# Attention and mixer kernel: batch 0's mixer as one stretch ahead of batch 2's attention, with seven products in all its blocks, and three of its x tiles in other buffers

## The chip, the cores and the metric

The kernel runs on 1 core of one Trainium2 chip. The metric is the device time of one execution in microseconds (us), given as the median of several runs. A core has five engines, each with its own instruction queue worked off in order: TensorE (PE in the profile, its weight loads PEld), VectorE (DVE), ScalarE (ACT), GpSimd (POOL) and SyncE (SP). In this kernel SP's queue issues every transpose by DMA and every store of the output; POOL's queue issues the loads of u, z, v and the weights.

## The reference

There are 8 batches of 3008 rows; u and v have 256 columns, z has 64. A gated attention makes x, and a mixer of two products in a row works on x:

```
scores = (z @ z.T) / 3008
x   = u * (maximum(scores, 0)**2 @ v)
h   = maximum(x.T @ w_tok1, 0) @ w_tok2          # 256 token features
u2  = x + h.T
out = u2 + maximum(u2 @ w_ch1, 0) @ w_ch2        # 1536 channel features
```

Nothing crosses from one batch to another, so the mixer of one batch may be done while the attention of a later one runs.

## The kernel before

**Tiles.** A batch is cut into six blocks q = 0 to 5 of 512 columns of rows (the last of 448), and its keys into six groups of four tiles of 128 rows. Operands are bf16; sums are in the eight banks of the PSUM, as slots of two banks that scores, attention sums, mixer products and their evacuations take in turn. A slot is free again when the instruction that empties it has run, on ScalarE or VectorE.

**Attention.** For a block and a key group, `score_run` (L465) multiplies two halves of z against each other at once; ScalarE takes relu to `at` (L491, L503), VectorE squares it (L511, L542). Scores are symmetric, so a group below the diagonal isn't computed again: `flip` (L562) lets SP transpose the `at` of its mirror image into a buffer `fl` (11 of them), and on the diagonal `flip_tiles` (L554) fills the lower triangle in three transposes within `at`. The attention's second product (L692, `acc`) uses `at` or `fl` as the moving side. Its two sums, one for each half of the 128 output rows, are joined by a copy on ScalarE and an add on VectorE (`cp`, L820, L826); the `gate` (L846, L851) multiplies by `uT`, the u rows transposed by SP (`turn_u`, L265, from `ur`), and writes x, transposed, to a tile `xT` (9 buffers). The planner issues a gate when `uT` has been asked for; the time of its landing isn't looked at.

**Mixer.** `turn_x` (L884, `x_pair`) turns x back by SP, `x_sums` (L921) makes sums and differences of it on VectorE, and the token product runs in seven products instead of eight (`tok1`, L1029, `a_ps`). VectorE collects it (`collect_a`, L1045 to L1063, `a_f`, `a_sb`), `tok2` (L1086, `h_ps`) makes h, and VectorE adds it into xT (L1095), from which SP makes `u_sb` (L1114). The channel half is `ch1` (L1143, `hp`), an evacuation with relu to `h2pre` (L1182 on ScalarE, L1184 on VectorE), and the second product in one of two forms. The plain one (`ch2`, L1366, `op`) is 48 matmuls of 128x256 a block, and VectorE adds u (L1383, `res`). The other first makes four sums of each four h2 tiles on VectorE (`make_sums`, L1223 to L1235, `hsum`) and then runs seven products of 12 matmuls of 128x128 each, 84 a block (L1280, `xb` and `zb`), which VectorE adds up into `ro` in seven adds (L1317). Which form a block takes is said by `fast(q)`: every block of batches 1 to 7 but the very last, and blocks 3 to 5 of batch 0, take the seven products.

**Order.** A planner written in the kernel emits the whole order of instructions. It goes through the attention's blocks, keeps a clock of each engine with assumed costs (a flip takes SP 2.2 us and lands 6.5 us after that, for example), puts pieces of the mixer (lists `heads` and `tails`) between the halves of the attention, and queues work for the other engines by the times that it assumes. `goals` says how far the mixer may go from the beginning of a block of the attention on; what it lets in is put ahead of that block's further work. A key (b, n) stands for step n of batch b's mixer: (0, 0) is batch 0's `tok1`, and (0, 4) lets in its `tok2` and the channel half of blocks 0 to 2. The before kernel lets batch 0's `tok1` in from batch 1's block 2 on, (0, 4) from batch 1's block 3 on, and the rest of batch 0 from batch 2's first block on. Loads are asked for by `at_group`, counted in key groups: those of z for batch 2 at the end of batch 1's block 2 (`ask_z`), each followed by its transpose `zT` (L141, L145). A load on POOL's queue waits behind a small marker operation (`mark`, L124) that holds it back until the work at that place has run.

Two rules of the before kernel concern only this place: in batch 1 the scores may not run further ahead than one block (`n = 0` in the main loop), and sums for the first seven-product block of a batch may be put off (`late_sums`).

Of the kernel before, what the change touches and what calls it, by code (L numbers as in the profile page):

```python
# [9 lines left out]
BF16 = mybir.dt.bfloat16  # L10
# [3 lines left out]
P = 128  # L14
QW = 512
# [42 lines left out]
def kernel(  # L58
# [12 lines left out]
    B, S, D = u.shape  # L71
# [7 lines left out]
    CHT = d_ch // P  # L79
    DT = D // P  # L80
# [288 lines left out]
    def has_room(names):  # L369
        return names() if callable(names) else all(live[n] < ROOM[n] for n in names)  # L370
# [279 lines left out]
    def do_whole(start, g):  # L650
        blk = cur[0]
        begins = blk.g is None
        if begins:
            blk.g, blk.half = g, 0
            blk.todo.remove(g)
            blk.slot += 1
            blk.parts.setdefault(g, 2 if g == LAST else 1)
            n = grain(blk.b, blk.q, g)
            tiles = list(range(GK - 1 if g == LAST else GK))
            blk.steps = [(dh, tiles[i:i + n]) for i in range(0, GK, n) for dh in range(DT)]  # L660
        final = blk.slot == NG
        if begins:
            if final and not blk.tails:
                do_tails(blk, max(start, tails_ready(blk)))
                start = pe[0]
        dh, tiles = blk.steps[blk.half]
        start, end = on_pe(start, "full", len(tiles) * column_time(blk.W))
        for i in tiles:
            whole_matmul(blk, g, i, dh, final and i == tiles[-1])
        if final:  # L670
            acc_free[dh] = push(
                "dve", end + 0.21, 0.61, 0.75,
                lambda t, dh=dh: gate(blk, dh, blk.acc[dh], t), first=1,
                room=("xT",) if dh == 0 else lambda: (blk.b, blk.q) in xTs)
        blk.half += 1
        if blk.half == len(blk.steps):
            blk.g = None
            finished(blk, g)
            if final:
                end_block(blk)  # L680
                if blk.q == WHOLE - 1:
                    ring.append((acc_free[-1], RING))
# [121 lines left out]
    def finish(blk, dh, end):  # L804


        W, acc = blk.W, blk.acc[dh]
        summed = Done()
        guess[blk.home[dh]] = end + 1.7
        ring.append((summed, blk.home[dh]))  # L810

        def load(e):
            return max(free[e], end) + sum(op.busy for op in waiting[e])

        on_act = blk.b > 0 or load("act") + 0.46 < load("dve") + 0.67

        def copy(t):
            cp = sb.tile([P, QW], F32, tag="res", name="cp", bufs=3)
            if on_act:
                nc.scalar.copy(cp[:, :W], acc[:, 1, :W])  # L820
            else:
                nc.vector.tensor_copy(cp[:, :W], acc[:, 1, :W])
            push("dve", t, 0.66, 0.78, lambda t: add(cp, t), first=1, done=summed)

        def add(cp, t):
            nc.vector.tensor_add(cp[:, :W], acc[:, 0, :W], cp[:, :W])  # L826
            push("dve", t, 0.58, 0.7, lambda t: gate(blk, dh, cp, t), first=1,
                 room=(lambda: (blk.b, blk.q) in uTs and has_room(("xT",))) if dh == 0
                 else lambda: (blk.b, blk.q) in xTs)

        engine, busy = ("act", 0.46) if on_act else ("dve", 0.66)
        push(engine, end + 0.21, busy, busy + 0.15, copy, first=1)

    gated = [0]

    def gate(blk, dh, acc, t):
        b, q, W = blk.b, blk.q, blk.W
        uT = uTs[b, q]
        if dh == 0:
            xTs[b, q] = sb.tile([P, DT, QW], BF16, tag="xT", name="xT", bufs=ROOM["xT"])  # L840
            live["xT"] += 1
            if W < QW:
                nc.gpsimd.memset(xTs[b, q][:, :, W:], 0.0)
        xT = xTs[b, q]
        full, rest = W // P, W % P
        nc.vector.tensor_mul(  # L846
            xT[:, dh, :full * P].rearrange("p (t s) -> p t s", s=P),
            acc[:, :full * P].rearrange("p (t s) -> p t s", s=P),
            uT[:, :full, dh, :])
        if rest:  # L850
            nc.vector.tensor_mul(  # L851
                xT[:, dh, full * P:W], acc[:, full * P:W], uT[:, full, dh, :rest])
        if dh == DT - 1:
            if b == 0 and q > 1:
                release("fl", [1], t)
            gated[0] += 1
            push("sp", t, 1.25, 7.5 if q < NQ - 1 else 12.0, lambda t: turn_x(b, q, t),
                 first=1 if b == 0 or q >= NQ - 2 else -1,
                 room=x_room(b, q), frees=fl_free if b and q % 2 == 0 else ())
# [139 lines left out]
    def add_mixer(b):  # L999
# [110 lines left out]
        def turn_u2(q, t):  # L1110
            live["us"] += 1
            turned_back[b] += 1
            us = sb.tile([P, DT, QW // P, P], BF16, tag="res", name="u_sb", bufs=3)
            nc.sync.dma_start_transpose(  # L1114
                out=us.rearrange("p h t d -> p (h t) d"),
                in_=xTs[b, q].rearrange("p h s -> p (h s)"))
            st["u", q] = us
            release("xT", xT_uses[q])
            for waits in st.pop(("waits", q), []):
                waits(t)  # L1120

# [8 lines left out]
        def ch1(q, c2, borrowed, end):  # L1130
# [28 lines left out]
            if (b, q, c2) == VERY_LAST:  # L1159
                landed, freed = [], Done()  # L1160

                def evacuate_part(r, t):
                    if r:
                        nc.scalar.activation(h2[:, r, :W], hps[1][:, r, :W], ACT.Relu)
                    else:
                        nc.vector.tensor_single_scalar(h2[:, r, :W], hp[:, r, :W], 0.0, AX.max)
                    landed.append(t)
                    if len(landed) == 2:
                        h2_done[q, c2].t = freed.t = max(landed)
                        keep_ends()  # L1170

                for r, engine, at, busy in ((0, "dve", end - 0.18, 0.62), (1, "act", end + 0.21, 0.5)):
                    push(engine, at, busy, busy + 0.16, lambda t, r=r: evacuate_part(r, t))
                ring.extend((freed, slot) for slot in slots)
                release("xT", xT_uses[q])
                return
            on_act = load("act") + 0.92 < load("dve") + 1.15 + (b > 0)

            def evacuate(t):
                recent[0] = h2[:, 0, :1]  # L1180
                if on_act:
                    nc.scalar.activation(h2[:, :, :W], hp[:, :, :W], ACT.Relu)  # L1182
                else:
                    nc.vector.tensor_single_scalar(h2[:, :, :W], hp[:, :, :W], 0.0, AX.max)  # L1184
                if q == NQ - 1:
                    keep_ends()
                if fast(q) and c2 % 2:
                    if borrowed and q == HALF and b < B - 1:
                        late_sums.append(lambda t: make_sums(q, c2 // 2, t))
                    else:  # L1190
                        make_sums(q, c2 // 2, t)
# [1 line left out]
            ring.append((push(engine, end + 0.21, busy, busy + 0.16, evacuate,  # L1193
                              done=h2_done[q, c2]), slots[0]))
            if c2 == CHT // 2 - 1:
                release("xT", xT_uses[q])

        def pairs_of(q):

# [146 lines left out]

        def fast(q):

            return (b > 0 or q >= HALF) and (b, q) != (B - 1, NQ - 1)

        def ch2(q, half, i, end):
            apart = alone(q, half)
# [138 lines left out]
    def next_piece(t):  # L1491
# [6 lines left out]
        for l in lists:  # L1498
            if not l:
                continue  # L1500
            p = l[0]
            if not p.urgent and p.key > goal[0]:
                continue
            if p.opens and not p.closes and opened and not (p.joins and joined[0]):
                continue
            r = max(t, known(*p.needs))
            if p.room and not has_room(p.room):
                r = FAR
            if p.slot:
                r = max(r, min(slots)) if slots else FAR  # L1510
            if r < FAR and r <= t + 0.05:
                return r, l
            if r < best[0]:
                best = r, l
# [79 lines left out]
            lambda: used.get((b, vorder[j]), 0) == NQ)  # L1594

    HALF = NQ // 2

    def ask_u(m, group):
        at_group(group, lambda: ask(lambda: u_then_turn(m), lambda: len(uTs) > m - 2))
# [6 lines left out]
    for b in range(B):  # L1606
# [15 lines left out]
                    at_group(base + NG + 4 + j // 3, lambda b=b, j=j: turn_next_z(b, j // 3))  # L1622
        else:
            if b == 1:
                ask_z(2, base + HALF * NG - 1)
            if b + 1 < B:
                last, m = base + NQ * NG - 1, (b + 1) * NQ
                ask_u(m, last)
# [102 lines left out]
    late_z(5, 9.0)  # L1731
    first_u(18.5)

    goals = {(1, 2): (0, 0), (1, HALF): (0, 1 + HALF)}
    for b in range(2, B):
        goals[b, 0] = (b - 1, 1 + HALF)
    done_units = 2
    NOW = 0.05
    STARVED = 0.7
# [3 lines left out]
    while cur[0] is not None or heads or tails:  # L1743
# [16 lines left out]
        runs = blk is not None and blk.whole  # L1760
        most = RING if runs else 1
        n = can_score(done_units, most)
        if n and blk is not None and blk.b == 1:
            b, q, _ = units[done_units][0]
            if b * NQ + q > NQ + blk.q + 1:
                n = 0
        slots = sorted(d.t for d, _ in ring if d.t is not None)
        n_now = min(n, len(slots))
        ts = FAR
# [115 lines left out]
```

## Time and profile before

| | |
|---|---|
| time, median of 3 runs | 1116.05 us (1115.90 to 1116.34) |
| the profiled execution | 1116.06 us |
| its span in the trace | 1114.0 us |
| TensorE busy | 1108.1 us, 10965 matmuls |
| VectorE busy | 780.5 us, 1855 instructions |
| ScalarE busy | 655.1 us, 817 instructions |
| GpSimd busy | 162.7 us, 382 instructions |
| mean granted clock of TensorE | 1.00 |

The span runs from the first instruction to the last in the trace; the execution lies some 2.1 us around it. Busy times are sums over the whole span. The mean duration of a pipelined matmul in the groups (375 ns for 512 columns) is longer than the time from its start to the next one's start, so the pace of a run of matmuls is read from the chain, which gives the length of a run and how many matmuls are in it. A row of the timeline gives the start, the length, the engine, the source line and what the instruction writes and reads; "SPq" is SP's queue. The length of a transpose there is that of its issue on SP, not of its transfer.

In the trace, batch 0's `tok1` begins at 110.4 us, its `tok2` at 127.8, and the plain channel half of blocks 0 to 2 runs from 134.8 to 166.0; then comes batch 1's attention from its block 3 on.

### The profile page before, as it was taken

How to read it: one execution, taken by the hardware profiler on the slowest of the kernel's cores; microseconds unless marked ns; L12 is line 12 of the kernel's file. 1: busy time of each engine (PE TensorE's matmuls, PEld its weight loads, DVE VectorE, ACT ScalarE, POOL GpSimd, SP SyncE). 2: the span in 40 equal slices, each digit the busy share in tenths (PEclk: the TensorE clock that was granted, in tenths of full speed). 3: DMA queues.
4: the chain of work that ended last, by engine and by line, in shares of the span. 5: the costliest groups of instructions: out<-in, count | busy, mean ns of one | idle time of the engine just before them, and what ended most of it. 6: DMA issues, size and time to landing. Idle time of an engine off the chain costs nothing.

```text
span 1114.0 us, 26933 instructions
## 1 busy us (share of the span) xinstructions
PE 1108.1 (99%) x10965; PEld 675.6 (61%) x10965; DVE 780.5 (70%) x1855; ACT 655.1 (59%) x817; POOL 162.7 (15%) x382
## 2 busy tenths in 40 slices
PE   9999999999999999999999999999999999999998
PEld 3444574666557665576555865557655576556676
DVE  6889846875758757588566885578756787557775
ACT  8999524645854458545675356653666536743354
POOL 5321100211003110031000311003200120000000
PEclk9999999999999999999999999999999999999999
DMA  9999955796987979779597897868968678585213
GB/s 178 173 183 157 208 117 114 124 179 135 183 137 142 187 126 185 142 141 209 128 174 132 143 197 144 168 121 158 191 156 172 109 157 174 128 160 99 63 58 95
DMA packets 466155, 165.51 MB, mean 149 GB/s; under 512 B 433072, under 2 KB 449008, under 8 KB 466032
## 3 DMA queue, kind: packets, MB, share of 16 engines
q1 hardware_dynamic: 436640, 131.11, 58.0%
q0 software_dynamic: 28880, 32.32, 20.6%
q8 instruction: 85, 1.39, 0.5%
q10 hardware_dynamic: 512, 0.38, 0.1%
q14 instruction: 38, 0.31, 0.1%
HBM read 65.40 MB, written 24.64 MB: 81 GB/s over the span
## 4 chain that ended last, share of the span: by engine, by line
PE 97%; DVE 1%; ACT 1%; issue 1%; POOL 0%; DVEq 0%; POOLq 0%; ACTq 0%
PE acc L692 41%; PE hp L1143 21%; PE xb L1280 10%; PE zb L1280 7%; PE sc L465 6%; PE h_ps L1086 4%; PE a_ps L1029 3%; PE op L1366 3%; PE first_acc L609 1%; DVE a_f L1045 0%; ACT h2pre L1182 0%; PE wp L205 0%; ACT at L503 0%; POOL hs L1156 0%; DVE at L511 0%
## 5 line engine op out<-in xcount | busy, mean ns | idle before, releaser
L1182 ACT ACTIVATE h2pre<-hp 128x1024 bf16<-128x1024 f32 (+1 forms) x277 | 269.4, 1007 | 257.8 <-PE hp L1143 165.3
L692 PEld LDWEIGHTS <-v_sb 64*128 64x128 bf16 x4418 | 238.0, 94 | 219.3
L692 PE MATMUL acc<-at,v_sb 64*128 64x512 bf16 (+1 forms) x2738 | 338.8, 374 | 0.0
L503 ACT ACTIVATE at<-sc 128x1024 bf16<-128x1024 f32 (+1 forms) x290 | 287.5, 1027 | 72.2 <-PE sc L465 65.4
L511 DVE TENSOR_TENSOR at<-at 128x1024 bf16<-128x1024 bf16 (+1 forms) x290 | 198.5, 687 | 110.7 <-ACT at L503 106.7
L1143 PE MATMUL hp<-xT,w_ch_sb 128*128 128x512 bf16 (+1 forms) x1152 | 273.5, 375 | 0.1
L692 PE MATMUL acc<-fl,v_sb 64*128 64x512 bf16 (+1 forms) x1680 | 191.4, 367 | 0.0
L1143 PEld LDWEIGHTS <-w_ch_sb 128*128 128x128 bf16 x1152 | 106.2, 98 | 99.8 <-issue 3.0
L465 PE MATMUL sc<-zT 64*128 64x512 bf16 (+1 forms) x732 | 131.3, 360 | 0.1
L1280 PEld LDWEIGHTS <-hsum 128*128 128x128 bf16 x1944 | 115.9, 98 | 17.6 <-issue 1.1
L1280 PEld LDWEIGHTS <-h2pre 128*128 128x128 bf16 x1458 | 89.1, 98 | 19.3 <-issue 1.2
L820 ACT COPY cp<-acc 128x512 f32<-128x512 f32 (+1 forms) x94 | 54.9, 584 | 71.4 <-PE acc L692 59.8
L826 DVE TENSOR_TENSOR cp<-acc,cp 128x512 f32<-128x512 f32 (+1 forms) x94 | 63.5, 675 | 42.3 <-ACT cp L820 41.8
L491 ACT ACTIVATE at<-sc 128x512 bf16<-128x512 f32 (+3 forms) x152 | 56.1, 444 | 45.4 <-PE sc L465 45.0
L1223 DVE TENSOR_TENSOR hsum<-h2pre 128x512 bf16<-128x512 bf16 (+1 forms) x132 | 52.2, 400 | 37.7 <-ACT h2pre L1182 35.9
L1280 PE MATMUL xb<-w_mix_sb,hsum 128*128 128x128 bf16 x972 | 68.6, 219 | 0.4 <-DVE ro L1317 0.3
L542 DVE TENSOR_TENSOR at<-at 128x512 bf16<-128x512 bf16 (+3 forms) x152 | 41.5, 321 | 38.3 <-ACT at L491 38.2
L1317 DVE TENSOR_TENSOR ro<-xb,u_sb 128x256 f32<-128x256 f32 (+1 forms) x132 | 52.6, 399 | 21.9 <-PE xb L1280 20.2
L465 PEld LDWEIGHTS <-zT 64*128 64x128 bf16 x732 | 42.0, 94 | 41.8 <-issue 3.8
L124 POOL CAST mark<-at 128x1 f32<-128x1 bf16 x24 | 8.9, 369 | 375.2 <-DVE at L511 375.2
L846 DVE TENSOR_TENSOR xT<-cp,uT 128x512 bf16<-128x512 f32 (+1 forms) x94 | 62.4, 664 | 0.8
L1095 DVE TENSOR_TENSOR xT<-xT,h_ps 128x1024 bf16<-128x1024 bf16 (+1 forms) x48 | 54.6, 1172 | 4.7 <-PE h_ps L1086 4.6
(89 smaller groups left out, 983.0 us busy)
## 6 DMA issues: line engine op xcount, KB each, us to landing
out_dram<-ro SPq DMA_DIRECT2D x37, 512.0 KB, 2.9
v_sb<-in_v_dram POOLq DMA_DIRECT2D x40, 256.0 KB, 4.6
ur<-in_u_dram POOLq DMA_DIRECT2D x40, 256.0 KB, 5.1
w_tok_sb<-in_moe_w_tok_dram POOLq DMA_DIRECT2D x10, 256.0 KB, 10.7
zs<-in_z_dram POOLq DMA_DIRECT2D x35, 64.0 KB, 3.7
at<-at SPq DMA_TRANSPOSE x114, 2.4
out_dram<-ro SPq DMA_DIRECT2D x7, 256.0 KB, 2.2
fl<-at SPq DMA_TRANSPOSE x105, 4.4
```

The costliest lines, as they stand in the source:

```text
L465: nc.tensor.matmul(sc[:, r, c0:c1], zT[h, k:k + P], zT[h, m + c0:m + c1], start=True, stop=True)
L491: nc.scalar.activation(a3[:, i, c0:c1], sc[:, r, c0:c1], ACT.Relu, scale=inv_S)
L503: nc.scalar.activation(view, sv, ACT.Relu, scale=inv_S)
L511: nc.vector.tensor_mul(view, view, view)
L692: nc.tensor.matmul(o, vs[blk.b, g][rows, i, dh * P:(dh + 1) * P], rhs, start=(dh, h) not in blk.begun, stop=stop, skip_group_check=True)
L820: nc.scalar.copy(cp[:, :W], acc[:, 1, :W])
L826: nc.vector.tensor_add(cp[:, :W], acc[:, 0, :W], cp[:, :W])
L846: nc.vector.tensor_mul(xT[:, dh, :full * P].rearrange("p (t s) -> p t s", s=P), acc[:, :full * P].rearrange("p (t s) -> p t s", s=P), uT[: ...
L1095: nc.vector.tensor_add(to, to, h[:, :, :n * P].rearrange("p h (s t) -> p h t s", t=n))
L1143: nc.tensor.matmul(hps[r % len(hps)][:, r, :W], w_ch1_sb[:, dc, cc * P:(cc + 1) * P], xT[:, dc, :W], start=(dc == 0), stop=(dc == DT - 1))
L1182: nc.scalar.activation(h2[:, :, :W], hp[:, :, :W], ACT.Relu)
L1280: nc.tensor.matmul(to[:, i * P:(i + 1) * P], lhs, weights[:, c2, :], start=(first_use and c2 == 0 and i == 0), stop=(c2 == CHT // 2 - 1), ...
```

## The change

- Batch 0's `tok1` is let in from batch 1's block 5 on, and all the rest of batch 0's mixer where batch 2's attention begins, as one stretch ahead of it. Batch 1's `tok1` is held back until the last block of batch 0's mixer.
- Blocks 0 to 2 of batch 0 take the seven products as well.
- Since all of batch 0's x has to be kept longer, three x tiles get another home: block 0's is the buffer `hs`, those of blocks 1 and 2 share one `fl` buffer (`x_kept`); the others stay in `xT`.
- The loads of z for batch 2 are asked for 13 key groups earlier (`Z2` = 4 instead of 17), and the rule that held batch 1's scores to one block ahead goes.
- Sums are put off only in batches 1 and up.

```diff
@@ -671,7 +671,7 @@
             acc_free[dh] = push(
                 "dve", end + 0.21, 0.61, 0.75,
                 lambda t, dh=dh: gate(blk, dh, blk.acc[dh], t), first=1,
-                room=("xT",) if dh == 0 else lambda: (blk.b, blk.q) in xTs)
+                room=xT_room(blk.b, blk.q) if dh == 0 else lambda: (blk.b, blk.q) in xTs)
         blk.half += 1
         if blk.half == len(blk.steps):
             blk.g = None
@@ -825,20 +825,53 @@
         def add(cp, t):
             nc.vector.tensor_add(cp[:, :W], acc[:, 0, :W], cp[:, :W])
             push("dve", t, 0.58, 0.7, lambda t: gate(blk, dh, cp, t), first=1,
-                 room=(lambda: (blk.b, blk.q) in uTs and has_room(("xT",))) if dh == 0
+                 room=(lambda: (blk.b, blk.q) in uTs and has_room(xT_room(blk.b, blk.q))) if dh == 0
                  else lambda: (blk.b, blk.q) in xTs)
 
         engine, busy = ("act", 0.46) if on_act else ("dve", 0.66)
         push(engine, end + 0.21, busy, busy + 0.15, copy, first=1)
 
     gated = [0]
+    x_kept = {}
+
+    def new_xT(b, q):
+
+        if b or q > 2:
+            xTs[b, q] = sb.tile([P, DT, QW], BF16, tag="xT", name="xT", bufs=ROOM["xT"])
+            live["xT"] += 1
+        elif q == 0:
+            hs = sb.tile([P, CHT, P], BF16, tag="hs", name="x_hs", bufs=1)
+            xTs[b, q] = hs.rearrange("p c s -> p (c s)")[:, :DT * QW].rearrange(
+                "p (h s) -> p h s", h=DT)
+        else:
+            if q == 1:
+                x_kept["fl"] = sb.tile(
+                    [P, 2, DT, QW], BF16, tag="fl", name="x_kept", bufs=ROOM["fl"])
+                live["fl"] += 1
+                fl_free.pop(0)
+            xTs[b, q] = x_kept["fl"][:, q - 1]
+
+    def xT_room(b, q):
+
+        return ("xT",) if b or q > 2 else ("fl",) if q == 1 else ()
+
+    x_kept_uses = [2]
+
+    def done_with_xT(b, q, uses):
+
+        uses[0] -= 1
+        if uses[0]:
+            return
+        if b or q > 2:
+            live["xT"] -= 1
+        elif q:
+            release("fl", x_kept_uses, pe[0] + 0.2)
 
     def gate(blk, dh, acc, t):
         b, q, W = blk.b, blk.q, blk.W
         uT = uTs[b, q]
         if dh == 0:
-            xTs[b, q] = sb.tile([P, DT, QW], BF16, tag="xT", name="xT", bufs=ROOM["xT"])
-            live["xT"] += 1
+            new_xT(b, q)
             if W < QW:
                 nc.gpsimd.memset(xTs[b, q][:, :, W:], 0.0)
         xT = xTs[b, q]
@@ -1115,7 +1148,7 @@
                 out=us.rearrange("p h t d -> p (h t) d"),
                 in_=xTs[b, q].rearrange("p h s -> p (h s)"))
             st["u", q] = us
-            release("xT", xT_uses[q])
+            done_with_xT(b, q, xT_uses[q])
             for waits in st.pop(("waits", q), []):
                 waits(t)
 
@@ -1172,7 +1205,7 @@
                 for r, engine, at, busy in ((0, "dve", end - 0.18, 0.62), (1, "act", end + 0.21, 0.5)):
                     push(engine, at, busy, busy + 0.16, lambda t, r=r: evacuate_part(r, t))
                 ring.extend((freed, slot) for slot in slots)
-                release("xT", xT_uses[q])
+                done_with_xT(b, q, xT_uses[q])
                 return
             on_act = load("act") + 0.92 < load("dve") + 1.15 + (b > 0)
 
@@ -1185,7 +1218,7 @@
                 if q == NQ - 1:
                     keep_ends()
                 if fast(q) and c2 % 2:
-                    if borrowed and q == HALF and b < B - 1:
+                    if borrowed and q == HALF and 0 < b < B - 1:
                         late_sums.append(lambda t: make_sums(q, c2 // 2, t))
                     else:
                         make_sums(q, c2 // 2, t)
@@ -1193,7 +1226,7 @@
             ring.append((push(engine, end + 0.21, busy, busy + 0.16, evacuate,
                               done=h2_done[q, c2]), slots[0]))
             if c2 == CHT // 2 - 1:
-                release("xT", xT_uses[q])
+                done_with_xT(b, q, xT_uses[q])
 
         def pairs_of(q):
 
@@ -1346,7 +1379,7 @@
 
         def fast(q):
 
-            return (b > 0 or q >= HALF) and (b, q) != (B - 1, NQ - 1)
+            return (b, q) != (B - 1, NQ - 1)
 
         def ch2(q, half, i, end):
             apart = alone(q, half)
@@ -1501,6 +1534,8 @@
             p = l[0]
             if not p.urgent and p.key > goal[0]:
                 continue
+            if p.key == (1, 0) and tails and tails[0].key < (0, 1 + NQ):
+                continue
             if p.opens and not p.closes and opened and not (p.joins and joined[0]):
                 continue
             r = max(t, known(*p.needs))
@@ -1594,6 +1629,7 @@
             lambda: used.get((b, vorder[j]), 0) == NQ)
 
     HALF = NQ // 2
+    Z2 = 4
 
     def ask_u(m, group):
         at_group(group, lambda: ask(lambda: u_then_turn(m), lambda: len(uTs) > m - 2))
@@ -1622,7 +1658,7 @@
                     at_group(base + NG + 4 + j // 3, lambda b=b, j=j: turn_next_z(b, j // 3))
         else:
             if b == 1:
-                ask_z(2, base + HALF * NG - 1)
+                ask_z(2, base + Z2)
             if b + 1 < B:
                 last, m = base + NQ * NG - 1, (b + 1) * NQ
                 ask_u(m, last)
@@ -1731,9 +1767,8 @@
     late_z(5, 9.0)
     first_u(18.5)
 
-    goals = {(1, 2): (0, 0), (1, HALF): (0, 1 + HALF)}
-    for b in range(2, B):
-        goals[b, 0] = (b - 1, 1 + HALF)
+    goals = {(b, 0): (b - 1, 1 + HALF) for b in range(2, B)}
+    goals[1, NQ - 1] = (0, 0)
     done_units = 2
     NOW = 0.05
     STARVED = 0.7
@@ -1760,10 +1795,6 @@
         runs = blk is not None and blk.whole
         most = RING if runs else 1
         n = can_score(done_units, most)
-        if n and blk is not None and blk.b == 1:
-            b, q, _ = units[done_units][0]
-            if b * NQ + q > NQ + blk.q + 1:
-                n = 0
         slots = sorted(d.t for d, _ in ring if d.t is not None)
         n_now = min(n, len(slots))
         ts = FAR
```

## The prediction

> **What bounds the kernel now.** The page's first part and the engine line of its chain of waits come first.
>
> ```profile
> PE 1108.1 (99%) x10965; PEld 675.6 (61%) x10965; DVE 780.5 (70%) x1855; ACT 655.1 (59%) x817; POOL 162.7 (15%) x382
> ...
> PEclk9999999999999999999999999999999999999999
> ...
> PE 97%; DVE 1%; ACT 1%; issue 1%; POOL 0%; DVEq 0%; POOLq 0%; ACTq 0%
> ```
>
> TensorE is busy for 1108.1 of 1114.0 us at full granted clock and is 97% of the chain. So a matmul taken away is a full gain, and a wait put in front of TensorE is a full loss: nothing later gives it back. The question is what the new order of matmuls costs in matmuls, and whether what feeds them can keep that order.
>
> The chain in order of time, in the old mixer stretch of batch 0 and in a block that already uses seven products, gives prices:
>
> ```profile
> 126.13 1.73 PE acc L692 x16
> ...
> 139.94 5.24 PE op L1366 x48
> 145.18 5.18 PE hp L1143 x24
> ...
> 201.54 2.75 PE hp L1143 x12
> 204.29 0.67 PE xb L1280 x12
> ```
>
> One attention matmul is 1.73/16 = 0.108 us, one plain channel matmul (`op`) 5.24/48 = 0.109 us, one product matmul 0.67/12 = 0.0558 us.
>
> The timeline of SP's queue, which issues every transpose, is the third view (start, length, tile, count):
>
> ```profile
> 106.27 12.99 SPq L562 DMA_TRANSPOSE fl<-at  x4
> 119.42 1.24 SPq L265 DMA_TRANSPOSE uT<-ur  x1
> 120.71 14.02 SPq L562 DMA_TRANSPOSE fl<-at  x5
> 134.85 2.83 SPq L1114 DMA_TRANSPOSE u_sb<-xT  x2
> 137.78 1.25 SPq L265 DMA_TRANSPOSE uT<-ur  x1
> ...
> 158.40 2.54 SPq L141 DMA_TRANSPOSE zT<-zs  x2
> ...
> 167.47 3.76 SPq L554 DMA_TRANSPOSE at<-at  x3
> 171.33 2.10 SPq L562 DMA_TRANSPOSE fl<-at  x1
> ```
>
> From 106 to 139 us the queue hardly rests. A small transpose takes 1.29 us from start to start (three `at` pieces: 167.47 to 171.33), a flip alone 2.1, four flips while u is loaded 13.15/4 = 3.3. Before the change nobody waits for this, because its mixer stretch (126 to 166 us) follows, where few transposes are asked for and the late ones are worked off.
>
> **The work, step by step.** Blocks 0, 1 and 2 of batch 0 lose 3 x 48 = 144 `op` matmuls: 144 x 0.1092 = 15.72 us. They gain 3 x 84 = 252 product matmuls: 252 x 0.0558 = 14.07. Net **-1.65 us**. The order of TensorE's instructions is the same for the first 937 matmuls (to 110.37 us, where `a_ps` began before) and for the last 9250 (from 201.54). In between, one stretch instead of two pieces takes away two changes between attention and mixer matmuls at about 0.1 us of idle each, and perhaps the 0.3 us for which `hp` waited at 201.54: together -0.5.
>
> VectorE gains 3 x (12 sums `hsum` + 7 adds `ro`, 0.42 us each) less the six `res` adds (0.69): +19.8 us in all, none on TensorE's path as long as VectorE stays ahead. A fast block is 5.18 + 84 x 0.0558 = 9.87 us of TensorE against 19 x 0.42 + 1.22 (the `u` add) = 9.2 of VectorE, so cover remains, 0.7 us a block. ScalarE's six `h2pre` of 1.0 us are covered too. The x tiles in `hs` and in one flip buffer add no instruction; they take one of 11 flip buffers for some 60 us. Priced at nothing; if a flip then waits for a buffer, that is in the transposes' lateness below. Output DMAs: three fewer in batch 0, no consumer.
>
> So far: profiled execution 1116.06 (span 1114.0, median of runs 1116.05) - 1.65 - 0.5 = **1113.9**, if TensorE never waits.
>
> **What SP's queue is asked for.** The attention of batch 1's blocks 2 to 4 now follows at once, 40 us earlier than the last of it did, and its flips, triangle pieces and u transposes with it; z of batch 2, whose `zT` stood at 143.9 to 162, now comes in the same stretch: six `zs` loads move ahead of the u loads on POOL's queue, five transposes on SP's. In order after the flip that began at 117.17 in the trace of before (the last one common to both orders): flip, `zT` x2, flip, flip, `at`, `zT` x3, flip, `at`, then flip **F** (for block (1,3)), `at`, flip, `at` x3, **U3** (uT of block (1,3)), `at` x3, **U4** (uT of block (1,4)). No such pile stands in the trace, so I add it up from rows:
> - F starts at 117.2 + 5 flips x 2.3 + 7 small x 1.29 + two u loads (993rd and 1031st matmul) at 2.2 each (the flip beside the load at 119.25 took 4.25 instead of 2.1) = **142**; with 2.1 per flip and 1 per load 138.7, with 2.4 and 3.3 per load 144.8. I take 141.5, since small transposes leave the DMA engines room for part of a load.
> - U3 is issued F + 2.1 + 1.29 + 2.1 + 3.87 = F + 9.4 and lands 3.0 later (row of `uT`: shortest 2.7, median 3.3): **153.9**.
> - U4 is issued 5.2 after U3, lands at 159.1. The next u load waits for U3's landing and then falls on it: 0 to 3 us, I take 1.5: **160.6**.
>
> **Who waits.** Block (1,3)'s gate stands in VectorE's order with its landing of U3, and (1,4)'s with U4; VectorE works in order, so all behind it waits too. Behind gate (1,3): the two `cp` adds that free the accumulators for block (1,5), whose first matmul would stand at 110.37 + (283 + 39) x 0.108 + 0.5 (nine small scores) + 84 x 0.0558 = 150.3 without waits. It can start at U3 + 2 gates x 0.69 + add 0.69 + 0.2 = 156.2. Behind gate (1,4): the last two sums of `a_f` that empty the bank of `tok1`, which the score after 28 more matmuls (153.0 without waits) takes: U4 + 2 x 0.69 + 2 x 0.42 + 0.1 = 162.9, so TensorE is **9.9 us** late there. Waits on the way (F itself wanted at 141.9, landing near 146; the second `zT` wanted at 138.4) are part of the 9.9, not added to it: SP and DMA run on while TensorE waits. After it, `tok2` (160.8 without waits) needs nothing further of SP, and TensorE is the bound again.
>
> Sum: 1113.9 + 9.9 = 1123.8. Bounds of the wait: from F at 138.7 with no load on U4, 138.7 + 17.6 + 2.3 - 153.0 = 5.6; from F at 144.8 and the whole load, 14.7. My sums leave TensorE no credit for transposes that overlap better than before, so I go 0.8 below and forecast **1123.0**.
>
> **Rivals.**
> - Transposes keep up: 1113.9. For it: in before nothing ever waited for a transpose, and the order gives U4 14 us from its place to its use. Against: in before SP ran 4 to 10 us behind its places with fewer of them in the stretch. The same case would be slower by 0.2% only from a wait of 4.3 us upward. Chance 0.13. (An edit that does not do what it says is out: the new order has the 252 products and the single stretch.)
> - SP catches up partly, a wait of 1.5 to 5 us at F or U3 only: F begins at 134.5 to 137, when flips and loads overlap fully. 1115.4 to 1118.9. Chance 0.14.
> - VectorE becomes the bound in the three new fast blocks: transposes in time, but x sums (8 x 0.29 us a block) come on top of 9.2 in 9.87, so TensorE waits 1 to 3 us: 1115 to 1117. Against: at 200 to 269 us VectorE is busy 76% with the same blocks, and the `hp` wait was 0.3. Chance 0.05.
> - A long wait also slows the clock: in the trace the granted clock is 1.00 throughout, but no wait of TensorE reached 1 us after the start, so no run here shows what several us do. If the matmuls after each of two such waits ran at half pace for as long as two passes of `acc` x16 (3.46 us), each would cost 1.7: 1123.0 + 3.4 = 1126.4. Chance 0.1. The Trainium skill (TensorE: Matmul & The Clock Gate, "Part 1: The HAM clock gate") states such a rule: about 3.4 us without matmuls bring the clock to half until some 3.4 us of them have run. By it the forecast would be near 1126; that is the rival just priced, and the trace neither bears it out nor speaks against it.
>
> **How the numbers follow.** Forecast (wait of 5 to 13 us) 0.58, keep up 0.13, partly 0.14, VectorE 0.05, clock 0.10. A measurement of this kernel can tell about 0.2%, 2.2 us: faster is below 1113.8, slower above 1118.3. Keep-up lies on the first edge: faster 0.07, same 0.06. Of partly, two thirds are same; VectorE is same. Faster 0.07, same 0.20, slower 0.73. The range 1115.3 to 1127.5 leaves out keep-up and the upper clock cases, under 0.2; the forecast's own is 1119 to 1127.
>
> **What would show it.** In the profile after, groups: `xb`/`zb` 252 matmuls more, `op` 144 fewer, PE busy 1.6 lower. SP's timeline from 106 to 165 us without a gap. DVE's `xT` (gate) with idle ahead, released by DMA `uT`; a gap of TensorE at about 142 to 160 before `acc` and `sc`, and none after. Wrong if those gates find uT landed, if SP has gaps before 140 us, or if the losses stand in the mixer stretch behind `hsum`.

## The result and the profile after

The changed kernel takes 1123.57 us (median of 6 runs, 1121.99 to 1129.55) against 1116.19 of the kernel before in the same runs: the ratio is 1.0071, 95% interval 1.0044 to 1.0098. It is slower, by 5 to 11 us. The profiled execution took 1121.99 us, its span is 1120.0, so 6.0 us more than before between the first instruction and the last. It is the fastest of the six executions; what the 1.6 us between it and the median are, its trace can't say.

The page after, engines and granted clock (the chain's share of TensorE is now 93%, with 3% for DMA):

```profile
PE 1105.4 (99%) x10999; PEld 679.7 (61%) x11073; DVE 787.8 (70%) x1899; ACT 662.6 (59%) x824; POOL 169.8 (15%) x382
...
PEclk9999899999999999999999999999999999999999
...
PE 93%; DVE 3%; DMA 3%; ACT 1%; issue 1%; SPq 0%; POOL 0%; DVEq 0%; ACTq 0%; POOLq 0%
```

The weight loads count the matmuls: 11073 against 10965, 252 products more and 144 `op` fewer; 74 records of matmuls themselves are missing from this trace. One digit of the clock row is 8, which no digit was before.

Where the 6.0 us come from is read by laying the weight loads of both kernels side by side, since no record of them is missing. At 109 us, where the order is still the same, they are 0.1 us apart. Where the common order begins again (201.5 us before, 208.5 after) the changed kernel is 7.0 behind; 0.7 of that comes back at 627 and 764 us, where the kernel before has two short waits that the changed one hasn't, and 0.3 at the end. With the 1.65 us of work saved, waits and what hangs on them cost some 8.6 us in between. Taking each matmul's time to the next one's start, less its pace (by the rows in the prediction 55.8, 109.2 and 215.8 ns for 128, 256 and 512 columns), places them: 0.6 in two waits at 109 and 111 us, **6.8 from 128 to 139**, 0.6 in two near 160, 0.9 at 193; the kernel before loses some 0.4 more than the changed one in the rest of the stretch. The large one is a wait and what follows it. TensorE's timeline of the kernel after, with what ended the wait in brackets:

```profile
127.59 1.04 PE L692 MATMUL acc<-at,v_sb 64*128 64x512 bf16 x8
132.58 0.58 PE L465 MATMUL sc<-zT 64*128 64x512 bf16 x2 [3.95 <-ACT at L503]
132.88 1.56 PE L692 MATMUL acc<-at,v_sb 64*128 64x512 bf16 x6
134.16 0.42 PE L465 MATMUL sc<-zT 64*128 64x256 bf16 x2
134.35 1.94 PE L692 MATMUL acc<-at,v_sb 64*128 64x512 bf16 x8
```

A score waits 4.1 us (128.45 to 132.58), and then eight `acc` matmuls take 1.94 us where they took 1.04. ScalarE's timeline shows whom it waited for:

```profile
126.52 0.55 ACT L491 ACTIVATE at<-sc 128x256 bf16<-128x256 f32 x2 [0.48 <-PE sc L465]
131.51 1.94 ACT L503 ACTIVATE at<-sc 128x1024 bf16<-128x1024 f32 x2 [4.44 <-DMA fl<-at]
```

The relu had its scores, but no `at` buffer to write to. There are six, and a buffer is free again only when the flip that reads it has landed. Between 100 and 172 us ScalarE waits 5.6 us for flips in all; in the kernel before it waits for none there. That flip is in SP's timeline, and the u load beside it in GpSimd's:

```profile
106.89 13.08 SPq L562 DMA_TRANSPOSE fl<-at  x5
120.14 2.55 SPq L141 DMA_TRANSPOSE zT<-zs  x2
122.81 8.03 SPq L562 DMA_TRANSPOSE fl<-at  x2
...
141.14 1.63 SPq L562 DMA_TRANSPOSE fl<-at  x1
...
149.72 2.14 SPq L265 DMA_TRANSPOSE uT<-ur  x1
...
155.83 1.26 SPq L265 DMA_TRANSPOSE uT<-ur  x1
```

```profile
118.70 0.57 POOL L255 DMA_DIRECT2D ur<-in_u_dram  x1 [0.33 <-issue]
122.80 0.54 POOL L255 DMA_DIRECT2D ur<-in_u_dram  x1 [0.33 <-issue]
```

The first of the two flips at 122.81 alone took SP 5.94 us and landed at 131.41; the u load issued at 122.80 landed at 128.94, and the one of 118.70 at 124.96. A flip alone took 1.63 (141.14). The windows of the same trace show the clock (columns: TensorE's busy time, weight loads, VectorE, ScalarE, GpSimd, granted clock, DMA share, GB/s):

```profile
130.00:132.00 2.00, 0.00 (x0) 0.00 (x0) 0.00 (x0) 0.49 (x1) 0.00 (x0) 0.89 1.16 207
132.00:134.00 2.00, 1.42 (x8) 0.81 (x9) 1.43 (x3) 1.88 (x3) 0.00 (x0) 0.50 0.57 128
134.00:136.00 2.00, 2.00 (x13) 0.89 (x10) 2.00 (x8) 1.10 (x4) 0.00 (x0) 0.50 1.22 163
...
138.00:140.00 2.00, 2.00 (x20) 0.99 (x18) 1.34 (x6) 0.16 (x1) 0.00 (x0) 0.90 0.66 148
```

The granted clock falls to 0.50 within the wait, at 131.56, and is back at 138.38. From 132.58 to 138.30 TensorE does work that takes 3.0 us at the pace of before; it takes 5.7. The half clock costs 2.7 us on top of the 4.1.

### The profile page after: what moved, and what is told of

Read it like the earlier page. It is cut to its first block, busy times and chain, and to the rows that moved or that the text cites. A ratio compares the mean times of both kernels' runs of the same rounds, so it can differ in the third digit from the quotient of the medians.

```text
span 1120.0 us, 27125 instructions
## 1 busy us (share of the span) xinstructions
PE 1105.4 (99%) x10999; PEld 679.7 (61%) x11073; DVE 787.8 (70%) x1899; ACT 662.6 (59%) x824; POOL 169.8 (15%) x382
## 4 chain that ended last, share of the span: by engine, by line
PE 93%; DVE 3%; DMA 3%; ACT 1%; issue 1%; SPq 0%; POOL 0%; DVEq 0%; ACTq 0%; POOLq 0%
PE acc L692 39%; PE hp L1176 21%; PE xb L1313 10%; PE zb L1313 8%; PE sc L465 6%; PE h_ps L1119 4%; PE a_ps L1062 3%; DMA fl<-at 1%; PE op L1399 1%; PE first_acc L609 1%; DVE at L511 1%; DMA uT<-ur 1%; DMA v_sb<-in_v_dram 1%; ACT at L503 1%; DVE a_f L1078 0%
## 5 line engine op out<-in xcount | busy, mean ns | idle before, releaser
L1215 ACT ACTIVATE h2pre<-hp 128x1024 bf16<-128x1024 f32 (+1 forms) x284 | 276.3, 1008 | 256.1 <-PE hp L1176 170.4
L692 PEld LDWEIGHTS <-v_sb 64*128 64x128 bf16 x4418 | 241.7, 94 | 217.8 <-issue 2.7
L1176 PE MATMUL hp<-xT,w_ch_sb 128*128 128x512 bf16 (+1 forms) x1020 | 254.4, 374 | 3.2
L1313 PEld LDWEIGHTS <-hsum 128*128 128x128 bf16 x2088 | 124.5, 98 | 19.3 <-issue 1.3
L1313 PEld LDWEIGHTS <-h2pre 128*128 128x128 bf16 x1566 | 95.6, 98 | 20.8 <-issue 1.2
L1256 DVE TENSOR_TENSOR hsum<-h2pre 128x512 bf16<-128x512 bf16 (+1 forms) x141 | 56.1, 402 | 38.5 <-ACT h2pre L1215 36.5
L1313 PE MATMUL xb<-w_mix_sb,hsum 128*128 128x128 bf16 x1044 | 73.6, 219 | 0.8 <-DVE ro L1350 0.8
L1350 DVE TENSOR_TENSOR ro<-xb,u_sb 128x256 f32<-128x256 f32 (+1 forms) x141 | 56.4, 400 | 22.5 <-PE xb L1313 20.6
L124 POOL CAST mark<-at 128x1 f32<-128x1 bf16 x29 | 13.1, 453 | 381.3 <-DVE at L511 381.1
L1268 DVE TENSOR_TENSOR hsum<-h2pre,hsum 128x512 bf16<-128x512 bf16 (+1 forms) x141 | 56.4, 400 | 2.2
```

Source lines behind the costliest of these rows:

```text
L692: nc.tensor.matmul(o, vs[blk.b, g][rows, i, dh * P:(dh + 1) * P], rhs, start=(dh, h) not in blk.begun, stop=stop, skip_group_check=True)
L1176: nc.tensor.matmul(hps[r % len(hps)][:, r, :W], w_ch1_sb[:, dc, cc * P:(cc + 1) * P], xT[:, dc, :W], start=(dc == 0), stop=(dc == DT - 1))
L1268: nc.vector.tensor_sub(kind(3), tiles_of(q, d, 1, 0), kind(1))
L1313: nc.tensor.matmul(to[:, i * P:(i + 1) * P], lhs, weights[:, c2, :], start=(first_use and c2 == 0 and i == 0), stop=(c2 == CHT // 2 - 1), ...
L1350: nc.vector.tensor_add(res(m, h), source, us(m, h) if opening else res(m, h))
```

## The experiments

The theory from this profile: SP's queue is late, as forecast, but it stops TensorE in more places than the two gates, because three kinds of buffers are free only when a transfer has landed (`at` by flips, the gates' cp tiles by uT, `ro` by stores). The waits stand side by side, and the one that ends last at each point counts. The rivals: the u loads alone; the early z alone; VectorE in the new fast blocks. The ratios are to the kernel before, run in between on the same chip, with 95% intervals. The spread of single runs is wide (the changed kernel's 7.6 us), so that a difference of two ratios under 0.2% tells little, and the trace decides more than the time.

**u_quarter and u_half.** In the load of u:

```diff
-        nc.gpsimd.dma_start(out=ur[:, :n, :], in_=rows_of(u[b], q))
+        if (b, q) in ((1, 3), (1, 4)):
+            nc.gpsimd.dma_start(out=ur[:, :1, :], in_=rows_of(u[b], q)[:, :1, :])
+            nc.gpsimd.memset(ur[:, 1:, :], 0.0)
+        else:
+            nc.gpsimd.dma_start(out=ur[:, :n, :], in_=rows_of(u[b], q))
```

(u_half: two tiles instead of one.)

> The changed kernel with the same order on TensorE, VectorE, ScalarE and SP; only the two u loads of batch 1's blocks 3 and 4 move a quarter of their bytes (the other three tiles of ur are set to zero, so this part of the output is left out). Theory: TensorE's wait of 4.13 us at 128.2 is ScalarE's relu waiting for an at buffer, which the flip issued at 122.81 holds until it lands at 131.4; the flip took 8.6 us because a u load ran beside it, and the half clock until 138 follows from the wait. Then the flip lands some 3 to 4 us earlier, the wait is under 1 us, no slice of the granted clock is under 1, and the time is 1115 to 1117. Rival 1, the two zT transposes put in front of the flip are the cause: the flip is still late by 2.5 us, wait 2 to 4 us. Rival 2, the wait comes from VectorE or ScalarE being behind: wait and clock unchanged, 1122 or more.

> As u_quarter, with half of the bytes of those two u loads (half of ur set to zero, so this part of the output is left out). Theory: the flip lands 1.5 to 2.5 us earlier, the wait at 128 is 1.5 to 2.5 us, and since it is shorter than 3.4 us the granted clock stays at 1.00: 1116.5 to 1119. Were the half clock tied to any wait, some matmuls after it would still run at half pace. Rivals as for u_quarter.

Measured: u_quarter 1.0055 (1.0035 to 1.0076), u_half 1.0071 (1.0052 to 1.0091): about as slow as the changed kernel. The trace tells why. TensorE's waits in u_quarter:

```profile
129.99 0.37 PE L469 MATMUL sc<-zT 64*128 64x512 bf16 x2 [0.77 <-ACT at L507]
160.33 0.41 PE L469 MATMUL sc<-zT 64*128 64x512 bf16 x2 [4.16 <-DVE a_f L1082]
```

The first part held: the wait at 128 fell from 4.1 to 0.9 us, since the flip took SP 2.67 us instead of 5.94. The two `zT` transposes still stood ahead of it, so rival 1 is out. The time didn't follow, because another wait took its place. VectorE's gates in the same run:

```profile
150.47 1.29 DVE L883 TENSOR_TENSOR xT<-cp,uT 128x512 bf16<-128x512 f32 x2 [3.41 <-DMA uT<-ur]
158.45 1.29 DVE L883 TENSOR_TENSOR xT<-cp,uT 128x512 bf16<-128x512 f32 x2 [4.37 <-DMA uT<-ur]
```

They wait for uT of (1,3) and (1,4), and the score that needs the bank of `tok1` behind them begins at 160.33; in the changed kernel it began at 161.22, in u_half at 161.06. It is nearly the same point in all three, whatever TensorE lost before, but not because SP's queue stood alike. SP issued the transpose for (1,4) 3.0 us earlier in u_quarter than in the changed kernel:

```profile
152.87 1.25 SPq L269 DMA_TRANSPOSE uT<-ur  x1
```

It landed at 158.43, 5.6 us after its issue instead of 3.5: the next u load, which waits for the landing of (1,3)'s uT, was issued in two parts from 150.93 on and landed at 154.75 and 157.40. A transpose beside a load is late once more; without that load it was not tried. A half clock of 3.4 us follows it now. My expectation of 1115 to 1117 had forgotten the second wait, which the prediction had. u_half shows the same, with a wait of 4.1 before 161.06; it lost the half clock at 128 but has it at 161. Its first wait came out at two of 0.7 and 0.9, each less than the 1.5 to 2.5 expected.

**uT_first and uT_first_u_quarter.** In the turn of u:

```diff
-            "sp", pe[0], 1.25, 5.0, lambda t: turn_u(m // NQ, m % NQ, t))))
+            "sp", pe[0], 1.25, 5.0, lambda t: turn_u(m // NQ, m % NQ, t), first=2 if m < 2 * NQ else 0)))
```

> The changed kernel with one edit: the planner puts the transposes of u for batch 1 ahead of other waiting transposes in SP's queue, so that uT of blocks (1,3) and (1,4) stands 5 and 12 operations earlier. Theory, two chains run side by side and the later one sets the end: the flip that holds ScalarE's at buffer (4.1 us and half clock) is in front of these operations and stays, only the 0.6 us at 160 go: 1120.5 to 1123. Rival, the gates' wait for uT is the cause and the wait at 128 only takes its place: the time falls by 3 us or more.

> Both edits together: u transposes first, and a quarter of the bytes in the u loads of blocks (1,3) and (1,4) (the rest of ur zero, that part of the output left out). Theory: u_quarter took away the wait at 128 and showed the one behind the gate of (1,4); uT_first takes that away too, so no wait of TensorE between 105 and 170 us is above 1.5 us, no half clock, 1115 to 1117.5. Rival, SP's queue is late by a fixed amount that always comes out somewhere: another wait of 3 us or more turns up before 170 us and the time stays above 1119.

Measured: uT_first 1.0081 (1.0055 to 1.0108), which speaks against the rival's fall of 3 us; its trace keeps a wait of 3.9 us behind a flip at 136.7. It has another of 3.3 at 108.2, which is not the edit's: the u loads of the start came late in this execution (see plain_blocks below). Both edits together: **1.0013 (0.9997 to 1.0030)**, 1119.27 us. Its timeline of TensorE has no wait above 1.2 us before 170 us and no half clock. What is left is 0.5 to 1.1 us each behind relus that wait for flips, and one new place:

```profile
129.69 0.37 PE L469 MATMUL sc<-zT 64*128 64x512 bf16 x2 [0.81 <-ACT at L507]
...
190.97 0.83 PE L1317 MATMUL xb<-w_mix_sb,hsum 128*128 128x128 bf16 x12 [2.07 <-DVE ro L1354]
```

So there are two waits side by side, each hidden by the other. Neither edit alone moves the time, and both together do, with intervals that don't meet: shown. The sum of 1115 to 1117.5 was missed by 2 us. That is the size of the last wait, in which VectorE sat idle for 1.7 us until the store of `ro` landed.

**z_late.** `Z2 = HALF * NG - 1` (17) instead of 4.

> The changed kernel with z of batch 2 asked for where the kernel before asks for it (17 key groups into batch 1 instead of 4): six z loads and five zT transposes leave the stretch before 140 us. Theory that the wait is made by all that stands in SP's queue before the flip: the flip moves up by the two zT (2.6 us), the wait falls to 0 to 2 us with no half clock, 1115.5 to 1118. Rival that the u loads alone make it: the flip still lands near 131, wait 3 to 4 us, 1120 to 1122. A later zT can make its own wait before batch 2's scores, which would show behind sc with a zT transpose as the releaser.

Measured: 1.0095 (1.0070 to 1.0119). As an experiment on one term it failed: the planner's order changes with it, into batch 3. Between 117 and 127 us there are waits of 1.6, 1.7 and 0.5 us behind flips, with no half clock, so the wait at 128 did become smaller, as the theory wanted; and up to 270 us TensorE lost some 5 us beyond its pace, where the changed kernel lost some 10. But 7.3 us are lost between 270 and 350 us, above all

```profile
318.12 1.04 PE L692 MATMUL acc<-fl,v_sb 64*128 64x512 bf16 x8 [3.20 <-DMA fl<-at]
```

where neither the kernel before nor the changed one waits. So a flip is late again in another place, and what early z costs alone stays open.

**old_order_new_homes.** The changed kernel with the old goals and the old `fast`; new homes, early z and no limit stay:

```diff
-    goals[1, NQ - 1] = (0, 0)
+    goals[1, 2] = (0, 0)
+    goals[1, 3] = (0, 1 + HALF)
-            return (b, q) != (B - 1, NQ - 1)
+            return (b > 0 or q >= HALF) and (b, q) != (B - 1, NQ - 1)
```

> Control: the changed kernel with the goals of the kernel before (tok1 from block 2 on, blocks 0 to 2 of batch 0 from block 3 on) and the plain form for them, but the new homes of the x tiles, z of batch 2 asked for early, and no limit on scores. Theory, what costs is the missing mixer stretch in the middle of batch 1 and not the homes (one flip buffer less) or the early z: as the kernel before within 1 us. Rival, early z or the missing flip buffer make the lateness: 2 us or more above the kernel before.

Measured: 1.0026 (1.0009 to 1.0042), 2.9 us. The rival holds, in part: a part of the loss (0.26% of 0.71%, both with wide intervals) comes with homes, early z and the missing limit even where the mixer stretch is back. The trace has `tok2` waiting 2.1 us at 132.6 for a relu that waits for a flip, and 0.5 at 110 likewise. The three edits were not taken apart.

**tok1_early.** `goals[1, 2] = (0, 0)` in place of `goals[1, NQ - 1]`.

> The changed kernel with one part undone: batch 0's tok1 is let in from batch 1's block 2 on, as in the kernel before (110 us), and the rest of its mixer stays where the change put it. Theory: tok1's 4.7 us of matmuls ask for no transpose and now stand before the flips that were late, so the wait at 128 shrinks to under 1 us; but tok1 no longer covers the time between the gate of (1,3) and the score behind it, so the wait for uT behind the gates comes out, 3 to 6 us at about 145 to 155, and half clock after it if it is above some 2.5 us: 1118 to 1123. Rival, that the 4.7 us are enough for all: 1114.5 to 1117.

Measured: 1.0045 (1.0027 to 1.0063). As the theory had it, the wait at 128 became smaller (1.4 and 0.5 us at 133 and 134, where under 1 was expected), and the gate's came out. TensorE and VectorE:

```profile
149.24 0.39 PE L465 MATMUL sc<-zT 64*128 64x512 bf16 x2 [3.93 <-DVE cp L826]
```

```profile
147.89 0.69 DVE L879 TENSOR_TENSOR xT<-cp,uT 128x512 bf16<-128x512 f32 x1 [4.57 <-DMA uT<-ur]
```

with 3.4 us of half clock after it.

**uT_first_z8, u_before_z, tok1_early_u_before_z.** Three tries at a version that has the products and not the waits: u transposes first and Z2 = 8; the same with Z2 = 7 and the two u loads 4 and 10 key groups earlier; that with `tok1` early.

> A whole kernel: u transposes first, and z of batch 2 asked for 8 key groups into batch 1 instead of 4, so that two zT transposes no longer stand before the flips at 983 and 1012 matmuls, nor z loads before 110 us. Theory: flips land 2.6 us earlier or more, uT comes in time, the largest wait is under 2.5 us with no half clock: 1115 to 1118.5. Rival as before: a wait of 3 us or more elsewhere, 1119 to 1124.

> A whole kernel with the new order and seven products, where the two u loads of blocks (1,3) and (1,4) are asked for 4 and 10 key groups earlier (before z of batch 2, which comes 3 groups later than in the changed kernel) and the u transposes of batch 1 go first in SP's queue. Theory: with no u load beside the flips after 110 us and uT in time, neither the wait at 128 nor the one at 160 remains and no half clock: 1114.5 to 1118; what is left are waits under 1.5 us, among them that of a product's sums for the store of the block before, near 190 us. Rival, SP's queue is too full in this order wherever the loads stand: a wait of 3 us or more, 1119 to 1124.

> A whole kernel: tok1 as in the kernel before, u transposes of batch 1 first in SP's queue, u loads of (1,3) and (1,4) before z of batch 2. Theory: both pushes work in one direction, every transpose after 110 us has 4 us or more to spare, no wait above 1.5 us before 190 us: 1114.5 to 1116.5, which is the seven products' 1.65 us less the waits near 190 us. Rival, lateness from before 110 us (u load beside flips at 92 to 107) takes the gain: 1117 to 1121.

Measured: 1.0051 (1.0032 to 1.0070), 1.0038 (1.0024 to 1.0053), 1.0048 (1.0029 to 1.0066). None beats the kernel before. In each, one wait of some 4 us stands in another place. In order, TensorE's largest wait:

```profile
147.91 3.60 PE L692 MATMUL acc<-fl,v_sb 64*128 64x512 bf16 x16 [3.73 <-DMA fl<-at]
```

```profile
121.33 1.89 PE L692 MATMUL acc<-fl,v_sb 64*128 64x512 bf16 x8 [3.82 <-DMA fl<-at]
```

```profile
191.50 1.02 PE L1313 MATMUL xb<-w_mix_sb,hsum 128*128 128x128 bf16 x12 [4.00 <-DVE ro L1350]
```

In the first two the rival held: a flip is late, only elsewhere. The last is of its own kind, and neither the theory nor the rival had it. No transpose stopped TensorE for more than 1.0 us there, as expected, but VectorE's add waits for the store of the block before:

```profile
191.02 0.42 DVE L1350 TENSOR_TENSOR ro<-xb,u_sb 128x256 f32<-128x256 f32 x1 [2.77 <-DMA out_dram<-ro]
```

That store was issued at 184.07 and landed at 190.90, 6.8 us against a median of 2.9, beside a v load of batch 2 (issued 183.74) and a transpose of u (184.48). `ro`, `hsum`, `fl` and two x tiles share the 11 buffers, so a new `ro` can have to wait for an old one to be stored. That the two x tiles are what makes the buffers short there was not tried.

**plain_blocks and u_before_z_plain.** The old `fast` in the changed kernel and in u_before_z.

> The changed kernel with blocks 0 to 2 of batch 0 in the plain form again, and all else as changed: prices the seven products alone. Theory: order and wait at 128 are unchanged (4 us and half clock), and TensorE has 1.65 us more work; less VectorE work in the stretch takes away about 1 us of waits at most: between the changed kernel's time and 2 us above it, 1122 to 1125. Rival, the new fast blocks make VectorE the bound: the time falls below the changed kernel's.

> As u_before_z, but blocks 0 to 2 of batch 0 in the plain form: prices the seven products where the transposes come in time. Theory by TensorE's work alone: 1.65 us slower than u_before_z. Less, or even faster, if the new fast blocks' sums and stores make waits of their own (0.9 to 2.2 us were seen near 190 us).

Measured: 1.0115 (1.0080 to 1.0150) and 1.0059 (1.0045 to 1.0073). Against the kernels with the products (1.0071 and 1.0038) the plain form is slower by 4.9 and 2.3 us, with intervals that also hold the 1.65 of the arithmetic. So no loss by the products is seen, and VectorE in the new fast blocks is not what makes the change slow. The first of the two profiles shows something else. SP's timeline in plain_blocks, and the same place in the changed kernel:

```profile
85.75 6.73 SPq L562 DMA_TRANSPOSE fl<-at  x1
92.53 2.13 SPq L265 DMA_TRANSPOSE uT<-ur  x1
```

```profile
85.82 1.63 SPq L562 DMA_TRANSPOSE fl<-at  x1
87.50 1.44 SPq L265 DMA_TRANSPOSE uT<-ur  x1
```

The order up to there is the same. In this execution the u loads behind the weights were issued at 69 and 70 us and landed at 91 and 93 (65.5, 67.2, 80 and 81 in the changed kernel's), the flip beside them took 5 us more, and the lateness went all the way through (its waits at 108.7, 137.9 and 168.1 are 2.7, 4.1 and 3.0 us). That execution took 1135.6 us, the longest of its four. The profiled executions of uT_first and u_before_z_plain are of the same kind: their loads were issued at 70 to 72 us and landed at 90 to 91, and the first long wait of TensorE in these three traces (2.2 to 3.3 us, ending at 107 to 109 us) stands in no trace whose loads had landed by 88 us. So a part of the spread of these kernels is when the loads of the start come in; the trace of one execution can't say how large a part.

## Why the prediction was right, and where its steps failed

The time, the sign and the cause in the large were right: 1123.0 forecast, 1123.57 measured, transposes that land too late for TensorE. The place of the main wait was wrong, and that the number fits so well is in part luck. By its steps:

- **The work, -1.65.** The counts are as foreseen, and the plain variants, 2.3 and 4.9 us slower with wide intervals, agree in sign; their intervals are too wide for the size.
- **SP's queue.** F was put at 141.5 and was issued at 141.14. U3 was to land at 153.9 and landed at 153.33; U4 at 160.6, it landed at 159.32. The rows of the queue came in the order that the prediction lists. That F fits to 0.4 us is luck, though: the last flip common to both orders began at 114.18 instead of 117.17 (a flip ahead of it had taken 5.15 us beside the u load of 105.70, which now comes later, and takes 2.52), and the stretch from there to F took 27.0 us where the sum has 24.3. Two errors of 3 us took each other away.
- **How late TensorE is.** The score behind gate (1,4) was to begin at 162.9 and began at 161.22, 8.2 us after its place without waits.
- **Where it waits: wrong.** The step that failed is "Waits on the way (F itself wanted at 141.9 ...)". I followed who reads a transpose and not who needs the buffer that it reads: the relu of the score at 127.37 writes to the `at` buffer that the flip issued at 122.81 holds, so TensorE stood at 128 us already. By the time U4 came it was so late that the wait for it cost 0.3; another 0.3 at 160.2 stands behind a relu. That early waits are part of the sum and not added to it was right, and u_quarter shows it: without the early wait, the same score begins at 160.33. It does so by the term "0 to 3 us, I take 1.5" for the next u load on U4: in u_quarter U4 landed 2.5 us later than the 3.0 after its issue that the sum counts.
- **The clock.** I gave the rival 0.1 and didn't count it; it happened and costs 2.7 us, as two stretches of half clock after one wait, where the rival had one after each of two. The early wait (4.1) and the clock (2.7) together with the small ones (0.6 at 109 to 112, 0.6 near 160, 0.9 at 193) come out near my 9.9 by luck of size: the wait was sized too high, the clock left out.
- **"Priced at nothing".** Two such prices failed. The `ro` adds wait for a store (VectorE idle for 1.7 us in uT_first_u_quarter and 2.8 in tok1_early_u_before_z), where I had written that output DMAs have no consumer: `ro` takes a shared buffer, and that makes the store's landing a consumer's matter. And homes, early z and the missing limit, without the new order, cost 2.9 us (interval 1.0 to 4.7).
- **VectorE: partly wrong.** The step "so cover remains, 0.7 us a block" leaves out the x sums of batch 1 that stand among the sums of these blocks. Only the rival counts them, and by its own rows a block then has 9.2 + 8 x 0.29 = 11.5 us of VectorE against 9.87 of TensorE. In the changed kernel VectorE doesn't pause for more than 0.1 us from 168 to 193.0 us:

```profile
180.00:185.00 5.00, 4.95 (x60) 3.70 (x60) 5.00 (x18) 3.10 (x4) 2.98 (x4) 1.00 0.61 107
185.00:190.00 5.00, 4.95 (x50) 3.37 (x50) 4.97 (x21) 3.12 (x4) 1.64 (x3) 1.00 0.47 103
```

  TensorE's 0.9 us at 193 are a wait for a `ro` add that VectorE began at 193.12. Its work ahead of that add ended at 193.00, and the store that had to land first landed at 193.00 too, so this wait is VectorE's lateness as much as the store's. The rival happened in part: 0.9 us, where it had 1 to 3.

## What to carry to other kernels

When a kernel is bound by one engine and the change packs its feeders, list for every transfer both who reads what it writes and who reuses what it reads, and take the slack of each; the shortest decides. Sum a serial queue from the durations in the trace, and expect that a transfer beside a large load takes longer (two to four times as long in these traces). Where several waits of equal cause stand one behind the other, taking one away may show nothing in the time: take them all away once, to see what is left to be gained, before looking for an order. Here even that, with a part of the u bytes not moved, left the kernel some 1.5 us slower than before (interval -0.3 to 3.4).

## What the runs showed of the hardware

**The clock changes on a grid of 3.41 us, and a part of one such stretch without matmuls is enough for it to fall.** The traces record when the granted clock changes. In each of them any two changes lie a whole number of times 3.413 us apart, whatever waits stand between: in the changed kernel 37 times (5.26 to 131.56 us), 2 times at half clock (to 138.38), and 288 times. So a trace can be cut into stretches of 3.413 us. For every stretch after 60 us, in all traces, the time of it in which TensorE waited, and the clock that followed:

| clock in the stretch | TensorE waited within it, us | clock in the next stretch |
|---|---|---|
| 1.00 | up to 2.0 (all other stretches) | 1.00 |
| 1.00 | 2.2 to 3.4 (13 stretches) | 0.50 |
| 0.50 | up to 0.7 (13 stretches) | 1.00 |
| 0.50 | 0.8 to 1.2 (3 stretches) | 0.50 |

So the length of a wait alone doesn't decide. One of 2.2 us that lay in a single stretch (u_before_z_plain, 104.7 to 106.9) was followed by half clock, and one of 3.2 us that fell on two (z_late, 314.9 to 318.1) was not. All nine waits of 3.8 us or more were, and the half clock then lasted 3.41 or 6.83 us; matmuls took twice their pace in it (some 430 ns from one pair of 512 columns to the next, instead of 216). What lies between 2.0 and 2.2, and between 0.7 and 0.8, no run shows.

The Trainium skill (TensorE: Matmul & The Clock Gate, "Part 1: The HAM clock gate") gives about 3.4 us without matmuls for the fall and about as much with matmuls for the return. These traces agree on the 3.4 us as the length of a stretch; but 2.2 us of waiting within one were enough for the fall, and up to 0.7 us of waiting didn't prevent the return.

**A load beside a transpose makes it much slower.** A flip of 512 KB took SP 1.6 us alone (137.71, 141.14 and 144.16 in the changed kernel) and landed 3.7 to 3.9 us after its issue. With a u load of 256 KB beside it, it took 5.95 at 92.51 and 5.94 at 122.81, and landed after 8.6; with a quarter of that load it took 2.67 in u_quarter and landed after 5.3. A store of 512 KB went from a median of 2.9 to 6.8 us beside a v load and a transpose.
